# Fused attention and experts: the later pairs' softmax reciprocals turned on VectorE and sent through DRAM instead of through TensorE

## Chip, cores and metric

One Trainium2 chip, one core. The metric is the device time of one execution in microseconds (us); smaller is better. The core has five engines, each with its own queue of instructions that is worked off in order: TensorE (PE in the profile, its weight loads PEld), VectorE (DVE), ScalarE (ACT), GpSimd (POOL) and SyncE (SP), which here only issues transfers.

## The reference, cut to what matters

```python
def _attn_ref(q, k, v, f):                       # 4 batches, 8 heads, 576 tokens, 64 dims
    scores = np.matmul(q, k.transpose(0, 1, 3, 2)) / np.sqrt(D)
    cum = np.cumsum(np.log(np.clip(f, 0.0001, 1.0)), axis=-1)
    scores = np.where(causal, -1e9, scores + cum[:, :, :, None] - cum[:, :, None, :])
    attn = np.exp(scores - np.max(scores, axis=-1, keepdims=True))
    attn = attn / (np.sum(attn, axis=-1, keepdims=True) + 1e-09)
    return np.matmul(attn, v)

def _moe_ref(x, domain_probs, w1, w2):           # 2304 tokens of 512, 4 experts of 1024
    p = domain_probs / (domain_probs.sum(-1, keepdims=True) + 1e-09)
    for e in range(4):
        out += p[:, e:e + 1] * (np.maximum(x @ w1[e], 0.0) @ w2[e])
```

The change concerns the division by the row sums. The kernel multiplies the unscaled product of the weights and v by the reciprocal of each query's sum. That product lies transposed, head dimension on the partitions and queries along the free axis, while the sums come with one query per partition, so the reciprocals have to be turned.

## The kernel before

Work is cut into "pairs" of two heads: 4 batches x 4 pairs x 2 halves of the queries (half 0: queries 0 to 255, half 1: queries 256 to 575) make 32 pairs, in the order of `JOBS` (L35). The four pairs of batch 0, half 0 are handled by the class `First` in a start-up phase written in a fixed order (`startup`, L1064). The other 28 (12 of half 0, 16 of half 1) are handled by `Job`, and their steps are interleaved with the expert steps: the main loop (L1166) records one expert step of a 256-token chunk after another and calls `pace` (L1052), which records attention steps up to a share of the work given by costs. A scheduler then sets each engine's final order; the order of recording alone doesn't fix it.

For one head of a pair, `head_steps` (L667) records: the split of the inputs in a high and a low part (`prep`), per tile of 128 queries the scores on PE, a running minimum on DVE and the exponential on ACT with the row sum as a by-product (`qk_tile`, L415), and one head later the turning of the weights (`tr`, L497: transposes on PE, high part copied by ACT at L475, low part by DVE at L482) and the product with v (`av`, L544: matmuls at L515, ACT copy `tmp` at L529, DVE sum `xs` at L537). After the second head of a pair, `recip` (L420) and later `fin` (L549) do the scaling:

- `recip`: DVE adds 1e-9 to the sums (L422) and takes the reciprocal (L425), 128 partitions x 4 or 6 values; POOL spreads each value to 64 columns (`rb`, L427).
- `fin` calls `spread` (L432): PE turns `rb` with one transpose per query tile (L437), two for half 0 and three for half 1, into a PSUM tile `b` out of the four of `ps_a`, which the scores, turned weights and products also use. Then DVE multiplies `xs` by `b` (L556 or L579), and the result is split into `xh` and `xl` (L562, L565) or written to `xf`.

```python
def spread(self):                                                  # L432
    ps = ps_a.tile([128, 512], F32, tag="a", name=f"b{self.nm}")
    for t in self.its:
        i, o = t - self.its[0], TOK0[t] - self.q0
        nc.tensor.transpose(
            ps[:, o : o + 128], self.rb[:, i].rearrange("p h d -> p (h d)"), ident
        )
    self.r = ps
```

The expert part consists of two sweeps over the chunks (`Step`, L748: first product L764, gate on ACT L775 and DVE L776, second product L794, weighted sum on DVE L816) and, at the end, 16 steps on the last four chunks together (`Big`, L921: L934, L960, L961, L992). Weights are split in a high part by ACT (L731) and a low part by POOL (L736). All transfers are issued by SP: weights L714, raw inputs L276, decay rows L295 read back from a DRAM tile `ncd` that was written at L200.

Of the kernel before, what the change touches and what calls it, by code (L numbers as in the profile page):

```python
# [8 lines left out]
F32 = mybir.dt.float32  # L9
F32R = mybir.dt.float32r  # L10
AF = mybir.ActivationFunctionType
ALU = mybir.AluOpType
# [57 lines left out]
def fused(ctx: ExitStack, tc: tile.TileContext, qk, v, f, probs, w, out):  # L70
# [33 lines left out]
    prob = const.tile([128, NT // 128, E], F32, name="prob")  # L104
    psum_ = const.tile([128, NT // 128, 1], F32, name="psum_")
    warm = const.tile([B * H, 1], F32, name="warm")
    ncd = dr_p.tile([B * H, 2, S], F32, tag="ncd", name="ncd", bufs=1)

    scr = acc_p.tile([128, 1024], F32, tag="acc", name="scr")
# [33 lines left out]
    def decays():  # L143
# [22 lines left out]
            channel_multiplier=1,  # L166
        )
        make_identity(nc, ident)
        for i in jobs[1:NPR]:
            nc.gpsimd.memset(i.kq[64:65, :, :CH], 8.0)  # L170
        for t in q2:
# [82 lines left out]
    class Job:  # L254
# [95 lines left out]
        def begin(self, hh):  # L350
            for t in self.its:
                self.p[hh, t] = p_p.tile([128, S], F32, tag="p", name=f"p{self.nm}_{hh}_{t}")
            self.nmax[hh] = st_p.tile([128, 8], F32, tag="nmax", name=f"nm{self.nm}_{hh}")
            if hh == 0:
                n = len(self.its)
                self.ssum = st_p.tile([128, 2, n], F32, tag="ssum", name=f"ss{self.nm}")
                self.rs = st_p.tile([128, 2, n], F32, tag="rs", name=f"rs{self.nm}")

        def qk_pe(self, hh, its):

# [59 lines left out]
        def recip(self):  # L420
            n, w_ = len(self.its), self.wq
            nc.vector.tensor_scalar(  # L422
                out=self.ssum, in0=self.ssum, scalar1=1e-9, scalar2=None, op0=ALU.add
            )
            nc.vector.reciprocal(out=self.rs, in_=self.ssum)  # L425
            self.rb = x_p.tile([128, 3, 2, D], F32, tag="r", name=f"rb{self.nm}")
            nc.gpsimd.tensor_copy(  # L427
                out=self.rb[:, :n],
                in_=self.rs.rearrange("p h i -> p i h").unsqueeze(3).to_broadcast([128, n, 2, D]),
            )  # L430

        def spread(self):  # L432

            ps = ps_a.tile([128, 512], F32, tag="a", name=f"b{self.nm}")
            for t in self.its:
                i, o = t - self.its[0], TOK0[t] - self.q0
                nc.tensor.transpose(  # L437
                    ps[:, o : o + 128], self.rb[:, i].rearrange("p h d -> p (h d)"), ident
                )
            self.r = ps  # L440

        def blocks(self):

# [28 lines left out]

        def tr_hi(self, hh, gi):
            ps, a0, first, at = self.tp[hh, gi]
            nc.scalar.activation(  # L475
                out=self.pt[hh][0][:, a0 : a0 + at - first], in_=ps[:, first:at], func=AF.Copy
            )

# [18 lines left out]
        def tr(self, hh, gi):  # L497
            self.tr_pe(hh, gi)
            self.tr_hi(hh, gi)
            self.tr_lo(hh, gi)  # L500

        def av_pe(self, hh):
            w_ = self.wq
# [45 lines left out]
        def fin(self):  # L549
# [1 line left out]
            pieces = place(self.b, self.half)  # L551
            k = self.pr
            direct = any(p[1] in DIRECT for p in pieces)
            self.spread()
            if direct:
                nc.vector.tensor_tensor(  # L556
                    out=self.xs[:, :w_], in0=self.xs[:, :w_], in1=self.r[:, :w_], op=ALU.mult
                )
            for d, c, o, n in pieces:
                if c in DIRECT:  # L560
                    th, tl = x_tiles(c)
# [9 lines left out]
                else:  # L571
# [4 lines left out]
                            out=xf[c][:, k, o : o + n], in_=self.xs[:, d : d + n]  # L576
                        )
                    else:
                        nc.vector.tensor_tensor(  # L579
                            out=xf[c][:, k, o : o + n],  # L580
                            in0=self.xs[:, d : d + n],
                            in1=self.r[:, d : d + n],
                            op=ALU.mult,
                        )


    class First(Job):
# [35 lines left out]
        def av_pe(self, hh):  # L623
# [3 lines left out]
            for jt, (a, z) in enumerate(((0, 256), (256, 384))):  # L627
# [4 lines left out]
                    start=(jt == 0),  # L632
                    stop=(jt == 1),
                )

        def spread_out(self):
            self.spread()
# [606 lines left out]
```

## Time and profile before

| what | value |
|---|---|
| median of 3 runs | 977.1 us (lowest 976.92, highest 1357.05) |
| the profiled execution's own time | 976.83 us |
| its span (first to last instruction) | 975.0 us, so 1.83 us lie around it |
| granted TensorE clock, mean | 0.999 of full speed |

The profile page gives per engine the busy time as a share of the span. A group of instructions is named by its line, engine and tile names; a wait names the instruction that waited and the one that released it. PE matmuls overlap in the records (each lasts longer than the step to the next one's start), so what one costs in the queue is read from the difference of start times.

### The profile page before, as it was taken

The numbers are of one execution on the slowest core, as the hardware profiler recorded it, in microseconds if no ns is written. First come the engines' busy times: TensorE is split into PE (matmuls) and PEld (weight loads), VectorE is DVE, ScalarE is ACT, GpSimd is POOL, SyncE is SP. The second block draws the span as 40 slices with busy tenths as digits, with TensorE's granted clock in tenths as the row PEclk, the third lists the DMA queues.
The fourth block names the chain that finished last, engine by engine and source line by source line (L and its number), as shares of the span: only waits on it lengthen the run. The fifth ranks groups of instructions, "written<-read, shape, count | busy, mean of one in ns | idle before, by whom it ended". The sixth has DMA issues, their size and how long they took to land.

```text
span 975.0 us, 15448 instructions
## 1 busy us (share of the span) xinstructions
PE 963.2 (99%) x5690; PEld 848.1 (87%) x5690; DVE 657.3 (67%) x1349; ACT 472.0 (48%) x979; POOL 413.0 (42%) x459
## 2 busy tenths in 40 slices
PE   8999999999999999999999999999999999999998
PEld 6898999899999999999899999988788888888886
DVE  6876565777867878877777563247866666566665
ACT  7776665566556656666556353234333232323220
POOL 4987763502303202204104083477654444555410
PEclk9999999999999999999999999999999999999999
DMA  7665331332412212313412022322211112111002
GB/s 258 255 207 163 118 106 49 103 109 69 137 52 90 102 54 84 120 52 96 150 57 66 23 66 83 113 86 66 87 44 44 44 43 69 62 44 44 23 0 87
DMA packets 29819, 85.87 MB, mean 88 GB/s; under 512 B 3160, under 2 KB 5264, under 8 KB 29744
## 3 DMA queue, kind: packets, MB, share of 16 engines
q1 hardware_dynamic: 29744, 84.89, 26.8%
q8 instruction: 45, 0.74, 0.3%
q14 instruction: 30, 0.25, 0.1%
HBM read 80.00 MB, written 4.87 MB: 87 GB/s over the span
## 4 chain that ended last, share of the span: by engine, by line
PE 87%; POOL 4%; DVE 3%; issue 2%; DMA 2%; ACT 1%; POOLq 0%; ACTq 0%; DVEq 0%
PE l L764 21%; PE l L794 20%; PE y L992 17%; PE m L934 13%; PE s L377 5%; PE t L465 5%; PE o L515 5%; POOL bwl L914 2%; DMA wr<-in_w 1%; POOL wt L891 1%; PE b L437 1%; POOL wl L736 1%; DVE kl L333 1%; DVE hi L339 0%; ACT wh L731 0%
## 5 line engine op out<-in xcount | busy, mean ns | idle before, releaser
L736 POOL TENSOR_TENSOR wl<-wr,wh 128x512 fp32r<-128x512 f32 x114 | 150.3, 1344 | 76.6 <-ACT wh L731 63.0
L764 PE MATMUL l<-xl,wh 128*128 128x256 f32 x640 | 182.0, 285 | 0.3 <-DVE xl L658 0.3
L764 PE MATMUL l<-xh,wh 128*128 128x256 f32 x640 | 181.2, 284 | 0.2 <-ACT xh L657 0.2
L764 PE MATMUL l<-xh,wl 128*128 128x256 f32 x640 | 181.3, 284 | 0.0
L816 DVE SCALAR_TENSOR_TENSOR acc<-y,prob,acc 128x512 f32<-128x512 f32 x120 | 88.3, 746 | 68.5 <-PE y L992 68.5
L406 ACT ACTIVATE p<-p,nm 128x576 f32<-128x576 f32 (+2 forms) x160 | 96.0, 600 | 64.8 <-DVE nm L391 64.3
L794 PE MATMUL l<-wh,gh 128*128 128x512 f32 x320 | 127.2, 398 | 0.0
L794 PE MATMUL l<-wl,gh 128*128 128x512 f32 x320 | 127.1, 397 | 0.0
L794 PE MATMUL l<-wh,gl 128*128 128x512 f32 x320 | 126.0, 396 | 0.0
L764 PEld LDWEIGHTS l<-xh,wh 128*128 128x128 f32 x640 | 120.5, 188 | 3.2 <-ACT xh L657 0.4
L764 PEld LDWEIGHTS l<-xl,wh 128*128 128x128 f32 x640 | 120.6, 188 | 3.0 <-DVE xl L658 0.5
L764 PEld LDWEIGHTS l<-xh,wl 128*128 128x128 f32 x640 | 120.5, 188 | 0.5
L325 POOL CAST q<-raw 64x320 fp32r<-64x320 f32 (+1 forms) x56 | 26.9, 480 | 210.3 <-PE s L377 181.9
L914 POOL TENSOR_TENSOR bwl<-wr,bwh 128x256 fp32r<-128x256 f32 (+1 forms) x80 | 78.5, 1009 | 80.5 <-ACT bwh L911 80.5
L391 DVE CUSTOM_DVE_ANT_0 p<-s,mask 128x288 f32<-128x288 f32 (+2 forms) x160 | 75.6, 477 | 43.3 <-PE s L377 39.7
L992 PE MATMUL y<-bwh,hh 128*128 128x512 f32 x256 | 101.1, 395 | 0.8 <-DVE acc L816 0.8
L992 PE MATMUL y<-bwl,hh 128*128 128x512 f32 x256 | 101.1, 395 | 0.0
L992 PE MATMUL y<-bwh,hl 128*128 128x512 f32 x256 | 100.4, 395 | 0.0
L776 DVE SCALAR_TENSOR_TENSOR gl<-l,gh 128x512 fp32r<-128x512 f32 x80 | 54.9, 686 | 54.6 <-ACT gh L775 54.4
L482 DVE TENSOR_TENSOR ptl<-t,pth 128x320 fp32r<-128x320 f32 (+2 forms) x120 | 65.3, 553 | 37.0 <-ACT pth L475 36.6
L934 PE MATMUL m<-rl,bwh 128*128 128x512 f32 x224 | 87.5, 390 | 0.0
L934 PE MATMUL m<-rh,bwh 128*128 128x512 f32 x224 | 87.3, 390 | 0.0
(117 smaller groups left out, 2077.5 us busy)
## 6 DMA issues: line engine op xcount, KB each, us to landing
wr<-in_w SPq DMA_DIRECT2D x96, 512.0 KB
raw<-in_qk SPq DMA_DIRECT2D x16, 896.0 KB
raw<-in_qk SPq DMA_DIRECT2D x12, 512.0 KB
vr<-in_v SPq DMA_DIRECT2D x16, 320.0 KB
out<-acc SPq DMA_DIRECT2D x16, 256.0 KB
vr<-in_v SPq DMA_DIRECT2D x8, 128.0 KB
first<-in_qk SPq DMA_DIRECT2D x3, 256.0 KB
first<-in_v SPq DMA_DIRECT2D x4, 128.0 KB
```

Source lines behind the costliest of these rows:

```text
L377: nc.tensor.matmul(out=ps[:, at : at + z - a], lhsT=lhsT, rhs=rhs, start=(m == 0), stop=(m == 1),)
L391: nc.vector.tensor_tensor_reduce(out=pt[:, a:z], in0=ps, in1=mask[:, m0 + a : m0 + z], scale=-0.125, scalar=BIG if n == 0 else nm[:, col : ...
L406: return nc.scalar.activation(out=pt[:, :w_], in_=pt[:, :w_], func=AF.Exp, scale=-1.0, bias=self.nmax[hh][:, c : c + 1], accum_out=self.ss ...
L482: nc.vector.tensor_tensor(out=lo[:, a0 + first : a0 + at - first], in0=ps[:, 2 * first : at], in1=hi[:, a0 + first : a0 + at - first].bitc ...
L736: eng.tensor_tensor(out=wl[n][:, a:z], in0=wraw[n][:, a:z], in1=wh[n][:, a:z].bitcast(F32), op=ALU.subtract)
L764: nc.tensor.matmul(out=self.l1p[:, fi, :], lhsT=lhsT, rhs=rhs[:, k, :], start=(k == 0 and m == 0), stop=(k == 3 and m == 2),)
L776: nc.vector.scalar_tensor_tensor(out=self.gl, in0=self.l1p, scalar=0.0, in1=self.gh.bitcast(F32), op0=ALU.max, op1=ALU.subtract,)
L794: nc.tensor.matmul(out=l2[tt], lhsT=lhsT, rhs=rhs, start=(self.ps == 0 and fi == 0 and m == 0), stop=(self.ps == 1 and fi == 1 and m == 2),)
L816: nc.vector.scalar_tensor_tensor(out=acc[c][:, tt, :], in0=ps, scalar=sc, in1=acc[c][:, tt, :], op0=ALU.mult, op1=ALU.add,)
L914: nc.gpsimd.tensor_tensor(out=lo[:, a:z], in0=x[:, a:z], in1=hi[:, a:z].bitcast(F32), op=ALU.subtract)
L934: nc.tensor.matmul(out=ps, lhsT=lhsT[:, o], rhs=rhs[:, k, :], start=(k == 0 and i == 0), stop=(k == 1 and i == 2),)
L992: nc.tensor.matmul(out=ps, lhsT=lhsT, rhs=rhs, start=(fi == 0 and m == 0), stop=(fi == 1 and m == 2),)
```

## The change

For the 28 later pairs the turning of the reciprocals leaves PE and POOL. `widen` has DVE write the 4 or 6 reciprocals per partition into the first columns of a constant 128 x 32 tile `rs32` (two of them, used in turn, filled with ones by POOL at the start), transpose it in blocks of 32 by 32 into `rt`, and ScalarE issues a transfer of `rt` to a DRAM tile `rd` in which all 128 queries of a head and query tile lie in a row. `fetch`, recorded after the last high-part copy of the second head's turned weights (`self.tail`), has ScalarE issue the read back: each head's row of 128 n values goes to 64 partitions of `r` in SBUF. `fin` then multiplies by `r`; since the third query tile overlaps the second by 64 queries, `scale` cuts at column 256 and half 1 pairs take a second instruction there. The four `First` pairs keep the old path.

```diff
--- before.py
+++ after.py
@@ -104,6 +104,7 @@
     prob = const.tile([128, NT // 128, E], F32, name="prob")
     psum_ = const.tile([128, NT // 128, 1], F32, name="psum_")
     warm = const.tile([B * H, 1], F32, name="warm")
+    rs32 = [const.tile([128, 32], F32, name=f"rs32_{n}") for n in range(2)]
     ncd = dr_p.tile([B * H, 2, S], F32, tag="ncd", name="ncd", bufs=1)
 
     scr = acc_p.tile([128, 1024], F32, tag="acc", name="scr")
@@ -166,6 +167,8 @@
             channel_multiplier=1,
         )
         make_identity(nc, ident)
+        for t in rs32:
+            nc.gpsimd.memset(t, 1.0)
         for i in jobs[1:NPR]:
             nc.gpsimd.memset(i.kq[64:65, :, :CH], 8.0)
         for t in q2:
@@ -354,7 +357,6 @@
             if hh == 0:
                 n = len(self.its)
                 self.ssum = st_p.tile([128, 2, n], F32, tag="ssum", name=f"ss{self.nm}")
-                self.rs = st_p.tile([128, 2, n], F32, tag="rs", name=f"rs{self.nm}")
 
         def qk_pe(self, hh, its):
 
@@ -422,22 +424,29 @@
             nc.vector.tensor_scalar(
                 out=self.ssum, in0=self.ssum, scalar1=1e-9, scalar2=None, op0=ALU.add
             )
-            nc.vector.reciprocal(out=self.rs, in_=self.ssum)
-            self.rb = x_p.tile([128, 3, 2, D], F32, tag="r", name=f"rb{self.nm}")
-            nc.gpsimd.tensor_copy(
-                out=self.rb[:, :n],
-                in_=self.rs.rearrange("p h i -> p i h").unsqueeze(3).to_broadcast([128, n, 2, D]),
-            )
-
-        def spread(self):
-
-            ps = ps_a.tile([128, 512], F32, tag="a", name=f"b{self.nm}")
-            for t in self.its:
-                i, o = t - self.its[0], TOK0[t] - self.q0
-                nc.tensor.transpose(
-                    ps[:, o : o + 128], self.rb[:, i].rearrange("p h d -> p (h d)"), ident
+            self.widen()
+
+        def widen(self):
+            n, x = len(self.its), rs32[self.pr % 2]
+            nc.vector.reciprocal(
+                out=x[:, : 2 * n].rearrange("p (h i) -> p h i", h=2), in_=self.ssum
+            )
+            rt = st_p.tile([128, 32], F32, tag="rt", name=f"rt{self.nm}", bufs=2)
+            nc.vector.transpose(out=rt, in_=x)
+            self.rd = dr_p.tile([32, 4, 32], F32, tag="rd", name=f"rd{self.nm}")
+            nc.scalar.dma_start(out=self.rd.rearrange("c b r -> b c r"), in_=rt)
+
+        def fetch(self):
+            n = len(self.its)
+            self.r = x_p.tile([128, 384], F32, tag="r", name=f"r{self.nm}")
+            with tc.issue_after(self.tail.ins):
+                nc.scalar.dma_start(
+                    out=self.r[:, : 128 * n],
+                    in_=self.rd[: 2 * n]
+                    .rearrange("(h i) b r -> h (i b r)", h=2)
+                    .unsqueeze(1)
+                    .to_broadcast([2, 64, 128 * n]),
                 )
-            self.r = ps
 
         def blocks(self):
 
@@ -472,7 +481,7 @@
 
         def tr_hi(self, hh, gi):
             ps, a0, first, at = self.tp[hh, gi]
-            nc.scalar.activation(
+            self.tail = nc.scalar.activation(
                 out=self.pt[hh][0][:, a0 : a0 + at - first], in_=ps[:, first:at], func=AF.Copy
             )
 
@@ -498,6 +507,8 @@
             self.tr_pe(hh, gi)
             self.tr_hi(hh, gi)
             self.tr_lo(hh, gi)
+            if hh == 1 and gi == len(self.blocks()) - 1:
+                self.fetch()
 
         def av_pe(self, hh):
             w_ = self.wq
@@ -551,11 +562,8 @@
             pieces = place(self.b, self.half)
             k = self.pr
             direct = any(p[1] in DIRECT for p in pieces)
-            self.spread()
             if direct:
-                nc.vector.tensor_tensor(
-                    out=self.xs[:, :w_], in0=self.xs[:, :w_], in1=self.r[:, :w_], op=ALU.mult
-                )
+                self.scale(self.xs, 0, w_)
             for d, c, o, n in pieces:
                 if c in DIRECT:
                     th, tl = x_tiles(c)
@@ -576,12 +584,17 @@
                             out=xf[c][:, k, o : o + n], in_=self.xs[:, d : d + n]
                         )
                     else:
-                        nc.vector.tensor_tensor(
-                            out=xf[c][:, k, o : o + n],
-                            in0=self.xs[:, d : d + n],
-                            in1=self.r[:, d : d + n],
-                            op=ALU.mult,
-                        )
+                        self.scale(xf[c][:, k, o : o + n], d, n)
+
+        def scale(self, out, d, n):
+            for a, z, o in ((d, min(d + n, 256), 0), (max(d, 256), d + n, 64)):
+                if a < z:
+                    nc.vector.tensor_tensor(
+                        out=out[:, a - d : z - d],
+                        in0=self.xs[:, a:z],
+                        in1=self.r[:, a + o : z + o],
+                        op=ALU.mult,
+                    )
 
 
     class First(Job):
@@ -632,6 +645,24 @@
                     start=(jt == 0),
                     stop=(jt == 1),
                 )
+
+        def widen(self):
+            rs = st_p.tile([128, 2, 2], F32, tag="rs", name=f"rs{self.nm}", bufs=2)
+            nc.vector.reciprocal(out=rs, in_=self.ssum)
+            self.rb = x_p.tile([128, 2, 2, D], F32, tag="r", name=f"rb{self.nm}")
+            nc.gpsimd.tensor_copy(
+                out=self.rb,
+                in_=rs.rearrange("p h i -> p i h").unsqueeze(3).to_broadcast([128, 2, 2, D]),
+            )
+
+        def spread(self):
+
+            ps = ps_a.tile([128, 512], F32, tag="a", name=f"b{self.nm}")
+            for i in range(2):
+                nc.tensor.transpose(
+                    ps[:, 128 * i : 128 * i + 128], self.rb[:, i].rearrange("p h d -> p (h d)"), ident
+                )
+            self.r = ps
 
         def spread_out(self):
             self.spread()
```

The scheduler sets the order anew. On PE, at the end of pair 1 of batch 0, half 1 (`o0_1_1_1` is its last product, `b0_1_1` the turned reciprocals, `l1` and `l2` are expert products, `t0_2_1` the next pair's weights being turned), the order before:

```order
L515 MATMUL o0_1_1_1_2894<-pth0_1_1_1_2791,v20_1_1_2269 128x192
L515 MATMUL o0_1_1_1_2894<-ptl0_1_1_1_2792,v20_1_1_2269 128x192
L515 MATMUL o0_1_1_1_2894<-pth0_1_1_1_2791,v20_1_1_2269 128x64
L437 MATMUL b0_1_1_2906<-ident_108,rb0_1_1_2732 128x128 x3
L764 MATMUL l1_1_0_1_1_4047<-xh1_620,wl34_3921 128x256
L764 MATMUL l1_1_0_1_1_4047<-xh1_620,wh34_3920 128x256
L465 MATMUL t0_2_1_0_0_2938<-ident_108,p0_2_1_0_2_2760 128x128
```

and now:

```order
L526 MATMUL o0_1_1_1_2900<-pth0_1_1_1_2795,v20_1_1_2272 128x192
L526 MATMUL o0_1_1_1_2900<-ptl0_1_1_1_2796,v20_1_1_2272 128x192
L526 MATMUL o0_1_1_1_2900<-pth0_1_1_1_2795,v20_1_1_2272 128x64
L474 MATMUL t0_2_1_0_0_2941<-ident_108,p0_2_1_0_2_2765 128x128
L474 MATMUL t0_2_1_0_0_2941<-ident_108,p0_2_1_0_3_2766 128x128
L825 MATMUL l2_0_7_2_0_0_3723<-wl29_2711,gh0_7_2_0_3620 128x512
L825 MATMUL l2_0_7_2_0_0_3723<-wh29_2710,gl0_7_2_0_3621 128x512
```

The row of three transposes is gone, and the products of the expert step that stand behind it are of an earlier step (sweep 0, group 7, chunk 2 instead of sweep 1, group 0, chunk 1). On ACT, from the exponential of this pair's last tile (`p0_1_1_1_4`) on, the order before (`wh` are weights being split, `tmp` a copy of a product):

```order
L406 ACTIVATE p0_1_1_1_4_2588,ss0_1_1_2428<-p0_1_1_1_4_2588,nm0_1_1_1_2589 128x576
L529 ACTIVATE tmp0_1_1_2756<-o0_1_1_0_2746 64x320
L406 ACTIVATE p0_2_1_0_2_2760,ss0_2_1_2764<-p0_2_1_0_2_2760,nm0_2_1_0_2763 128x384
L731 ACTIVATE wh34_3920<-wr34_3176 128x1024
L731 ACTIVATE wh35_3927<-wr35_3287 128x1024
L475 ACTIVATE pth0_1_1_1_2791<-t0_1_1_1_0_2793 128x512
L475 ACTIVATE pth0_1_1_1_2791<-t0_1_1_1_1_2816 128x384
L475 ACTIVATE pth0_1_1_1_2791<-t0_1_1_1_2_2854 128x320
L406 ACTIVATE p0_2_1_0_3_2761,ss0_2_1_2764<-p0_2_1_0_3_2761,nm0_2_1_0_2763 128x512
L775 ACTIVATE gh1_0_1_0_3970<-l1_1_0_1_0_3934 128x512
```

and now, with the write of the turned reciprocals (`rd0_1_1`) and the read (`r0_1_1`):

```order
L408 ACTIVATE p0_1_1_1_4_2591,ss0_1_1_2433<-p0_1_1_1_4_2591,nm0_1_1_1_2592 128x576
L806 ACTIVATE gh0_7_2_0_3620<-l1_0_7_2_0_3582 128x512
L540 ACTIVATE tmp0_1_1_2761<-o0_1_1_0_2751 64x320
L408 ACTIVATE p0_2_1_0_2_2765,ss0_2_1_2769<-p0_2_1_0_2_2765,nm0_2_1_0_2768 128x384
L437 DMA rd0_1_1_2737<-rt0_1_1_2735 4x32x32
L484 ACTIVATE pth0_1_1_1_2795<-t0_1_1_1_0_2797 128x512
L484 ACTIVATE pth0_1_1_1_2795<-t0_1_1_1_1_2820 128x384
L484 ACTIVATE pth0_1_1_1_2795<-t0_1_1_1_2_2858 128x320
L443 DMA r0_1_1_2864<-rd0_1_1_2737 128x1x384
L408 ACTIVATE p0_2_1_0_3_2766,ss0_2_1_2769<-p0_2_1_0_3_2766,nm0_2_1_0_2768 128x512
L806 ACTIVATE gh0_7_2_1_3719<-l1_0_7_2_1_3649 128x512
```

The write stands behind the gate, one copy and one exponential of the next pair, the read right behind the three copies of turned weights (`pth0_1_1_1`); two weight splits that stood there before have moved elsewhere.

## Rows read from the trace of the kernel before

**Rows 1.** The page's head and busy time of each engine.

```profile
span 975.0 us, 15448 instructions
...
PE 963.2 (99%) x5690; PEld 848.1 (87%) x5690; DVE 657.3 (67%) x1349; ACT 472.0 (48%) x979; POOL 413.0 (42%) x459
```

**Rows 2.** Busy time by stretch; columns: stretch, its length, engines, clock, DMA share, GB/s.

```profile
30.00:100.00 70.00, 69.12 (x474) 63.33 (x474) 54.27 (x127) 50.09 (x112) 60.31 (x69) 1.00 0.57 189
100.00:180.00 80.00, 80.00 (x558) 74.04 (x557) 46.01 (x123) 47.88 (x118) 47.07 (x57) 1.00 0.29 86
...
700.00:800.00 100.00, 100.00 (x434) 81.30 (x433) 63.58 (x92) 30.01 (x52) 49.93 (x55) 1.00 0.16 53
```

**Rows 3.** Waits of PE; columns: who <- whom, us in total, times, longest.

```profile
PE b L437 <- POOL rb L427: 1.1, 1, 1.1
PE y L992 <- DVE acc L816: 0.8, 1, 0.8
PE o L515 <- DVE ptl L482: 0.7, 1, 0.7
PE s L377 <- DVE nm L391: 0.5, 1, 0.5
```

**Rows 4.** PE in order of time around the `b` of a half 1 pair; columns: start, length.

```profile
248.46 0.55 PE L437 MATMUL b<-ident,rb 128*128 128x128 f32 x3
248.77 0.36 PE L764 MATMUL l<-xh,wl 128*128 128x256 f32 x1
248.97 0.28 PE L764 MATMUL l<-xh,wh 128*128 128x256 f32 x1
249.09 0.38 PE L465 MATMUL t<-ident,p 128*128 128x128 f32 x2
```

**Rows 5.** The same around the `b` of a half 0 pair.

```profile
204.58 0.41 PE L437 MATMUL b<-ident,rb 128*128 128x128 f32 x2
204.74 0.37 PE L764 MATMUL l<-xh,wl 128*128 128x256 f32 x1
204.94 0.28 PE L764 MATMUL l<-xh,wh 128*128 128x256 f32 x1
```

**Rows 6.** Groups by line; columns: operation, tiles, count, busy us, mean ns, idle before.

```profile
L437 PE MATMUL b<-ident,rb 128*128 128x128 f32 x80 | 15.2, 286 | 1.1 <-POOL rb L427 1.1
...
L565 DVE TENSOR_TENSOR xl<-xs,xh 128x256 fp32r<-128x256 f32 x16 | 8.5, 530 | 2.1 <-ACT xh L562 1.9
...
L425 DVE RECIPROCAL rs<-ss 128x4 f32<-128x4 f32 (+1 forms) x32 | 5.7, 179 | 1.4
```

**Rows 7.** Transfers issued by SP: nanoseconds of an issue, shortest, median, longest.

```profile
L295 SPq DMA_DIRECT2D kl<-ncd x56: 221/251/443, 20.2 to 513.7; - x56
...
L276 SPq DMA_DIRECT2D raw<-in_qk x28: 545/546/612, 11.9 to 505.8; - x28
```

**Rows 8.** The chain of work that ended last, its first transfer: start, length.

```profile
0.73 1.91 DMA scr<-in_f
```

**Rows 9.** SP's queue in order of time: a write to DRAM and its read back.

```profile
14.55 0.31 SPq L200 DMA_DIRECT2D ncd<-scr  x1
...
20.17 0.53 SPq L295 DMA_DIRECT2D kl<-ncd  x2
```

**Rows 10.** ACT in order of time for the pair of rows 4.

```profile
236.87 0.19 ACT L406 ACTIVATION_READ_ACCUMULATOR p<-p,nm 128x1 f32 x1
...
241.04 1.53 ACT L475 ACTIVATE pth<-t 128x512 fp32r<-128x512 f32 x3
```

**Rows 11.** DVE in order of time for the same pair.

```profile
238.69 0.17 DVE L425 RECIPROCAL rs<-ss 128x6 f32<-128x6 f32 x1
...
251.59 0.49 DVE L537 TENSOR_TENSOR xs<-o,tmp 64x320 f32<-64x320 f32 x1
```

**Rows 12.** DVE in order of time, one instruction at 460 us.

```profile
460.06 4.30 DVE L333 TENSOR_TENSOR kl<-raw,hi 64x576 fp32r<-64x576 f32 x1 [0.80 <-ACT hi L324]
```

**Rows 13.** POOL in order of time at the same place.

```profile
459.96 3.77 POOL L736 TENSOR_TENSOR wl<-wr,wh 128x512 fp32r<-128x512 f32 x3
```

## Prediction

> **What bounds the kernel now.** I read the page's head and busy times first [rows 1]: PE is busy 963.2 of 975.0 us, the next engine, DVE, 67%. That alone doesn't prove a bound, since matmul records overlap, so next came the busy time by stretch [rows 2]: from 30 us on PE loses at most about 0.9 us in a stretch, at clock 1.00, whether DVE and ACT are loaded to 78% and 72% (30 to 100 us) or less (58% and 60% from 100 to 180). Third, the waits of PE [rows 3]: the longest entries are 1.1, 0.8, 0.7 and 0.5 us, once each. Fourth, PE in order of time [rows 4, 5]: one instruction starts as soon as the one ahead lets it. So the program is one long queue on PE with almost no holes, and a change is worth what it takes out of that queue, less the holes it makes. The other engines count only where they get so late that PE has to wait.
>
> **The change part by part.** The sum is made against the profiled execution, 976.83 us (span 975.0 and 1.83 around it).
>
> *Transposes off PE.* 28 pairs lose their `b` transposes: 12 pairs with two, 16 with three, 72 of the 80 in the group of line 437 [rows 6]. The mean of 286 ns in that row is the length of a record, not what it takes from the queue; the starts tell that. In a half 1 pair three transposes start at 248.46, and the second expert product behind them starts at 248.97; one product takes 0.12 (248.97 to 249.09), so the three take 248.97 - 248.46 - 0.12 = 0.39 us, in which the slower change from transposing back to products is contained [rows 4]. In a half 0 pair it is 204.94 - 204.58 - 0.12 = 0.24 us [rows 5]. The sum: 16 x 0.39 + 12 x 0.24 = 6.2 + 2.9 = 9.1 us off PE. All of it lies on the queue that sets the end, so I take it whole: -9.1. Where a transpose of weights follows directly, some of the price of changing stays; that makes it a little less, not another case.
>
> *POOL.* 28 copies `rb` go, and two small fills come at the start; POOL is at 42% and nobody but PE waited for these copies, for 1.1 us in one case [rows 1, 3]. That one is in the start-up phase, where the four `First` pairs stay as they are. Zero.
>
> *DVE.* 28 block transposes come. The trace shows none; the nearest rows are the reciprocal at 179 ns and a two-input product over 256 columns at 530 ns [rows 6], and I take 0.2. The multiplication now reads `r` in SBUF in place of PSUM, and half 1 pairs get a second piece. With 0.2 to 0.5 us more for each of some 70 instructions DVE gets 14 to 35 us more of 975, and goes from 67% to about 70%. Off the path.
>
> *ACT.* Two issues per pair, 56 in all. SP's issues take 0.25 us (two rows, median) to 0.55 us (128 partitions, two heads) [rows 7]; 56 times that is 14 to 31 us of ACT's queue, spread over the 527 us between 30 and 557. In the stretch 100 to 180 ACT goes from 60% to about 65%. What stands behind an issue in the queue are exponentials, copies of turned weights and the gates; a gate is needed only after the next step's 24 products (24 x 0.12 = 2.9 us), which covers one issue several times. Zero, with up to 31 us if nothing covered it.
>
> *The write's wait.* ACT stands at the write until the block transpose is done. In the pair shown the sums were complete at 237.06 (236.87 + 0.19) and the reciprocal at 238.86 [rows 10, 11]; the transpose ends some 0.3 later, and in the new order a gate, a copy and an exponential of the next pair stand between on ACT. Hidden but for some tenths.
>
> *The read's wait.* ACT stands at the read until the write has landed. No row shows a write of this size. A read of 2 KB took 1.91 us from the start of its issue [rows 8]; that is the lower bound. A 72 KB write issued at 14.55 held back its own read until 20.17, 5.6 us, with larger loads under way [rows 9]; the upper. From the reciprocal's end at 238.86 to the end of the last turned weights at 242.57 (241.04 + 1.53) there are 3.7 us [rows 10, 11]. I take the value nearest to the smaller transfer, some 2.2 with the issue: it is over when ACT reaches the read. With 5.6 ACT would stand 2 us in each pair, which is the second rival.
>
> *The read's landing.* From 242.57 to the end of the last sum `xs` at 252.08 (251.59 + 0.49) are 9.5 us in which the read has to arrive [rows 10, 11]; with the same bounds it does. The Trainium skill (DMA: Bandwidth & Descriptors, section on why a DMA increments its semaphore by 16) speaks against this read: the number of DMA engines is the largest up to 16 that divides the first dimension on both sides, here 2 for two heads. By its 436 GB/s for all 16, an estimate for 192 KB on two is 2.0 + 3.6 = 5.6 us in place of 2.4. No run here shows it yet; by the one and by the other the 9.5 us hold, and only the second rival's chance is raised by it.
>
> *A denser order.* Beside the 72 transposes the new order runs attention ahead: at the pair shown, PE's queue stands in an expert step five places earlier than before. The half 0 pairs thus get closer together, roughly to what the stretch from 30 to 100 us looks like, where PE lost 0.88 us in 70 [rows 2]. From 100 to 180 us it lost nothing. I add 80 / 70 x 0.88 = +1.0. Below is zero (DVE and ACT may keep up), above the first rival.
>
> *DVE behind POOL.* A DVE product with both inputs in SBUF lasted 4.30 us, until 464.36, while three POOL products ran until 463.73 [rows 12, 13]; soon after it PE waited 0.5 us for the minimum `nm` [rows 3]. The new scaling is such a two-input product, 28 pairs and the second pieces. I add one further wait of the longer kind, 0.7 [rows 3]. The Trainium skill (SBUF — State Buffer, section on who interferes with whom) says that a DVE instruction with two SBUF inputs is blocked for a whole GpSimd instruction that reads SBUF, and the reverse; the trace agrees, with 4.30 us. With PSUM as one input, as `b` was, it doesn't apply, so the rule speaks against this part; read strictly it could strike at each of the new products, and then the first rival is where it leads.
>
> Sum: 976.83 - 9.1 + 1.0 + 0.7 = 969.4 us. The median is 0.27 above the profiled execution, so 969.7.
>
> **The rivals.**
> 1. *The gain is eaten by density.* If all of 30 to 557 us ran with the losses of the stretch 30 to 100, PE would lose 527 / 70 x 0.88 = 6.6 us [rows 2] in place of the 1.0: 976.83 - 9.1 + 6.6 + 0.7 = 975.0. For it: ACT and DVE both get more work, in less time. Against it: from 100 to 180 us neither is above 60%, and PE's lead over the gates is a whole step.
> 2. *ACT stands at the read and PE waits (slower).* It holds the read until the write has landed, and gates, exponentials and turned weights queue behind it. It decides from the point at which a write takes longer than the 3.7 us of rows 10 and 11. With the 5.6 of rows 9 ACT stands 2 us in each pair; if PE then waits as long as in its longest wait for a late vector result, 0.7 [rows 3], it is 28 x 0.7 = 19.6: 976.83 - 9.1 + 19.6 = 987.3. For it: a queue in order, and 28 round trips through DRAM. Against it: rows 9 come from the start, when all inputs are loaded; later the DMA share is 0.29 and 0.16 [rows 2].
> 3. *The late waits go too.* The order is new, so the waits of 0.7 and 0.5 need not come again, and the added 1.7 neither: 976.83 - 9.1 - 1.2 = 966.5.
>
> **How the numbers follow.** Chances: the forecast 0.58, rival 1 0.20, rival 2 0.15, rival 3 0.07. The range 964.5 to 980 holds the forecast and rivals 1 and 3 with a little on either side and leaves out most of rival 2. 2% is about what a measurement of this kernel can tell from no change, and it is 19.5 us: faster than 957.6 would need more than the transposes and all waits since 30 us together, 0.01; slower than 996.6 only a rival 2 with 1 us of PE per pair, 0.04; within 2% 0.95.
>
> **What would show it.** Right: PE has 72 fewer instructions of line 437 and its busy time is about 9 us less, with no new entry above 1 us among PE's waits; ACT's waits for the write are under 1 us a pair; DVE's scaling doesn't wait for the read. Wrong: a row in which ACT waits for the transfer of `rd` by microseconds, many times, with PE waiting for `gl` or `ptl` behind it; scaling instructions of 2 us and more beside POOL's; or a time that is lower by less than 5 us although no wait on PE has grown, which would mean that the transposes cost less than the starts say.

## The result and the profile after

The changed kernel takes 983.55 us (median of seven, 980.59 to 988.49) against 978.95 for the kernel before in the same comparison: the ratio is 1.0053, 95% interval 1.0027 to 1.0078 (a ratio of means, in which one execution of the kernel before that took 1357.05 us is left out). It is slower by about 5 us where 7.4 us less had been forecast (969.4 against 976.83). The profiled execution is the slowest of the seven (988.49 us), so its waits are somewhat larger than usual.

The page's head and busy times of the changed kernel, against [rows 1]:

```profile
span 986.7 us, 15439 instructions
...
PE 969.9 (98%) x5618; PEld 852.3 (86%) x5618; DVE 667.9 (68%) x1393; ACT 469.4 (48%) x979; POOL 398.7 (40%) x433
```

The 72 transposes are gone (5690 to 5618 instructions), and yet PE is busy for longer. Busy time by stretch, against [rows 2]:

```profile
30.00:100.00 70.00, 66.88 (x448) 60.34 (x447) 55.30 (x115) 45.93 (x101) 56.00 (x60) 1.00 0.61 196
100.00:180.00 80.00, 76.53 (x513) 70.71 (x513) 54.70 (x150) 49.57 (x132) 45.54 (x56) 0.96 0.32 101
700.00:800.00 100.00, 100.00 (x434) 81.37 (x433) 66.57 (x96) 30.97 (x54) 50.52 (x56) 1.00 0.17 54
```

From 30 to 180 us PE got through 961 matmuls where before it got through 1032, with 6.6 us idle instead of 0.9, and the granted clock fell to 0.96 in the second stretch. From 700 to 800 us PE does the same as before. Between the end of the attention and there the place of the tiles tells, of which more below. PE's waits, against [rows 3]:

```profile
PE o L526 <- DVE ptl L491: 3.2, 3, 2.3
PE l L795 <- ACT xh L570: 2.0, 1, 2.0
...
PE b L662 <- POOL rb L653: 1.1, 1, 1.1
PE t L474 <- ACT p L408: 1.0, 2, 0.5
PE t L474 <- DVE nm L393: 0.8, 1, 0.8
```

The new entries are late results of DVE (turned weights, minima) and ACT (scaled activations, exponentials), not the transfers themselves. The transfers show one step further back. The two lines that issue them (nanoseconds: shortest, median, longest), the write first:

```profile
L437 ACTq DMA_DIRECT2D rd<-rt x28: 539/540/1113, 49.7 to 557.4; - x28
```

```profile
L443 ACTq DMA_DIRECT2D r<-rd x28: 535/536/562, 52.8 to 561.7; - x28
L443 ACTq EVENT_SEMAPHORE  x22: 17/17/2449, 64.8 to 561.6; - x22
```

Each of the 56 issues takes ACT 0.54 us in the median, 30.9 us in all. The gaps on ACT right in front of the 28 reads add up to 12.8 us, 2.46 us in the longest. ACT stands in front of the writes as well: 27 of the 28 are issued 0.03 us after the block transpose that they wait for has ended, and the gaps in front of them add up to 19.8 us, 3.68 us in the longest, and are above 1 us in eight. The longest, on ACT and then on DVE:

```profile
475.42 0.58 ACT L806 ACTIVATE gh<-l 128x512 fp32r<-128x512 f32 x1
479.69 0.54 ACTq L437 DMA_DIRECT2D rd<-rt  x1
...
479.46 0.20 DVE L435 STREAM_TRANSPOSE rt<-rs 128x32 f32<-128x32 f32 x1
```

How long the transfers are shows in the chain of work that ended last (start, length):

```profile
63.86 4.20 DMA rd<-rt
84.95 7.16 DMA r<-rd
95.13 4.08 DMA rd<-rt
99.28 4.56 DMA r<-rd
...
278.47 5.32 DMA rd<-rt
...
347.62 8.59 DMA r<-rd
...
409.31 5.71 DMA rd<-rt
415.12 8.37 DMA r<-rd
```

On this chain, which holds seven of the writes and four of the reads, a write needs 3.9 to 5.7 us from its issue, a read 4.6 to 8.6. The longest wait on PE, at 77 us, looks like this on DVE and POOL in order of time:

```profile
74.94 2.59 DVE L315 TENSOR_TENSOR v<-vb,v 128x128 fp32r<-128x128 f32 x2
77.45 1.83 DVE L592 TENSOR_TENSOR xs<-xs,r 128x256 f32<-128x256 f32 x1
79.32 0.56 DVE L491 TENSOR_TENSOR ptl<-t,pth 128x384 fp32r<-128x384 f32 x1
...
71.04 6.34 POOL L767 TENSOR_TENSOR wl<-wr,wh 128x512 fp32r<-128x512 f32 x5
...
77.75 1.25 POOL L767 TENSOR_TENSOR wl<-wr,wh 128x512 fp32r<-128x512 f32 x1
```

The new multiply of line 592 lasts 1.83 us beside POOL (0.42 in the median), and the turned weights for which PE stands come right behind it. At 103 us it is ACT, and then the clock:

```profile
103.00 0.38 PE L474 MATMUL t<-ident,p 128*128 128x128 f32 x2
105.41 0.50 PE L795 MATMUL l<-xh,wh 128*128 128x256 f32 x2 [2.03 <-ACT xh L570]
```

```profile
103.00:115.00 12.00, 9.42 (x49) 8.66 (x48) 5.93 (x19) 6.04 (x19) 3.17 (x6) 0.72 0.24 71
115.00:127.00 12.00, 12.00 (x84) 11.10 (x83) 7.56 (x23) 8.95 (x19) 9.91 (x11) 1.00 0.48 153
```

Behind that stall of 2.0 us, and another of 0.5 us at 106 us, PE ran at its lower level, 1.2 GHz, until about 113 us (a 256-column product takes 0.21 us from start to start instead of 0.12); the mean granted clock of the 12 us is 0.72.

So four suspects stood: the scheduler's new order, the multiply beside POOL, the round trip through DRAM, and, from the fourth experiment on, something that slows the expert matmuls.

### The profile page after: what moved, and what is told of

Read it like the earlier page. It is cut to its first block, busy times and chain, and to the rows that moved or that the text cites. A ratio compares the mean times of both kernels' runs of the same rounds, so it can differ in the third digit from the quotient of the medians.

```text
span 986.7 us, 15439 instructions
## 1 busy us (share of the span) xinstructions
PE 969.9 (98%) x5618; PEld 852.3 (86%) x5618; DVE 667.9 (68%) x1393; ACT 469.4 (48%) x979; POOL 398.7 (40%) x433
## 4 chain that ended last, share of the span: by engine, by line
PE 76%; DVE 10%; DMA 6%; issue 3%; ACT 2%; POOL 1%; ACTq 0%; DVEq 0%; POOLq 0%
PE y L1023 17%; PE l L825 16%; PE l L795 16%; PE m L965 14%; PE s L379 4%; PE t L474 4%; PE o L526 3%; DMA rd<-rt 3%; DMA r<-rd 3%; DVE wl L767 1%; DVE v L315 1%; DVE p L393 1%; DVE ss L424 1%; DVE acc L847 1%; PE s L608 1%
## 5 line engine op out<-in xcount | busy, mean ns | idle before, releaser
L795 PE MATMUL l<-xh,wh 128*128 128x256 f32 x640 | 183.7, 288 | 2.0 <-ACT xh L570 2.0
```

Source lines behind the costliest of these rows:

```text
L795: nc.tensor.matmul(out=self.l1p[:, fi, :], lhsT=lhsT, rhs=rhs[:, k, :], start=(k == 0 and m == 0), stop=(k == 3 and m == 2),)
```

## The experiments

Ratios are to the kernel before, with 95% intervals; a difference of two ratios is put into us by 978.4, its median. To hold an engine to an order, each of its instructions was tied behind its forerunner in a list taken from the other kernel, with an edge that orders issue alone:

```diff
+            for a, z in zip(order, order[1:]):
+                tc.add_manual_dep(z, a.name, NOSYNC, reason="in_order")
```

No run does this to a kernel with its own order and changes nothing else. The nearest is e6 below, the changed kernel in its own order without one of its waits, which stands within 0.0004 of it.

**e1, e2: order and work exchanged.**

> The changed kernel's operations, with every engine held to the order that the kernel before had (the 72 transposes and the 28 copies on GpSimd simply missing from it); only the 56 transfers on ScalarE's queue are placed by the scheduler. Theory order (the closer order of batch 1's attention takes away the slack in front of PE): the 9.1 us of the transposes come back nearly whole, ratio to before 0.990 to 0.994, about 969 to 972 us. Theory lock (VectorE's multiply now reads two SBUF operands and stands behind GpSimd): the 56 multiplies are all still there, so ratio 1.003 to 1.006. Theory round trip (write 4 to 6 us, read 5 to 9 us, VectorE and ScalarE held): the trips are as long as before and only somewhat better covered, ratio 0.999 to 1.004.

> The other half of the crossing: the operations of the kernel before (transposes on PE, widening on GpSimd, factors in PSUM, no round trip), with every engine held to the changed kernel's order; the 72 transposes and 28 GpSimd copies are placed by the scheduler. Theory order: about as much is lost as the changed kernel lost beyond its gain, 10 to 14 us, ratio to before 1.010 to 1.015. Theory lock and theory round trip: neither is in this kernel, ratio 0.998 to 1.003.

e1: 1.0126 (1.0107 to 1.0146). e2: 1.0058 (1.0041 to 1.0074). The new order, with none of the new work, costs the old work 5.7 us (its 72 transposes and 28 copies placed by the scheduler): theory order was right on e2 in its direction, with a number about twice too large. But the old order doesn't help the new work, it makes it worse, which none of the theories had. ACT and then PE in order of time in e1 show one place where it does:

```profile
98.33 0.54 ACTq L683 DMA_DIRECT2D rd<-rt  x1
...
103.83 0.55 ACTq L689 DMA_DIRECT2D r<-rd  x1
104.42 0.51 ACT L654 ACTIVATE p<-p,nm 128x256 f32<-128x256 f32 x1 [4.11 <-DMA rd<-rt]
...
105.07 0.44 PE L721 MATMUL t<-ident,p 128*128 128x128 f32 x2 [1.87 <-ACT p L654]
```

The write is issued at 98.33, the read stands until it has landed, and ACT is idle for 4.11 us before the exponential behind the read, for which PE waits 1.9 us.

**e3 to e5: without the transfers.** In e3 and e5 `fetch` sets `self.r = one`, an SBUF tile of ones, and both transfers go; e3 in the new order, e5 in the old. e4 is e3 with one operand:

```diff
-                    nc.vector.tensor_tensor(
+                    nc.vector.tensor_scalar(
                         out=out[:, a - d : z - d],
                         in0=self.xs[:, a:z],
-                        in1=self.r[:, a + o : z + o],
-                        op=ALU.mult,
+                        scalar1=0.001,
+                        scalar2=None,
+                        op0=ALU.mult,
```

> The changed kernel in the changed kernel's own order, without the 28 writes and 28 reads: the multiply takes its second operand from an SBUF tile of ones instead (the softmax division is left out; reciprocal and block transpose stay). Theory round trip: what the trips hold up is gone, about 969 to 974 us, ratio to before 0.990 to 0.995. Theory order and theory lock: the order and the multiply with two SBUF operands are as in the changed kernel, ratio 1.002 to 1.006.

> As the run without transfers, in the same order, and the multiply is by a constant: one SBUF operand instead of two (the softmax division is left out). Theory lock: faster than the run without transfers by 3 to 10 us, and the slow multiplies (up to 1.83 us beside GpSimd in the changed kernel) fall to 0.2 to 0.4 us. Theory order and theory round trip: the same as the run without transfers within 2 us.

> The changed kernel's operations in the order of the kernel before, without the 28 writes and 28 reads (the multiply takes a tile of ones; the softmax division is left out). It closes the square of order and transfers: new order with transfers 1.0053, old order with transfers 1.0126, new order without 1.0006. Theory round trip (the transfers are what makes the old order slow): it falls by 12 us or more, ratio 0.990 to 0.998. Theory order as first put (the old order has the slack in front of PE): 3 to 6 us below the new order without transfers, 0.994 to 0.997. If what slows both orders is the multiply or the missing transposes themselves, it stays above 1.003.

e3: 1.0006 (0.9996 to 1.0016); e4: 0.9993 (0.9981 to 1.0005); e5: 1.0005 (0.9991 to 1.0019). The transfers cost 4.6 us in the new order and 11.8 in the old. The second operand is worth 1.3 us as measured, with intervals that overlap, where theory lock had 3 to 10, so it isn't the main cause. With e5 theory order falls in its first form: the old order is no better for the new work than the new one. What none of the theories had: 72 transposes less and no transfers, and still no gain.

**e6, e7: the two waits apart.** e6 keeps all 56 transfers but multiplies by `one`; e7 drops the writes and reads constant rows.

```diff
-                        in1=self.r[:, a + o : z + o],
+                        in1=one[:, a + o : z + o],
```

> The changed kernel in its own order with all 56 transfers as they are, but VectorE's multiply takes a tile of ones and so waits for no read (the softmax division is left out). Only ScalarE is still held, at each read's issue until its write has landed. Theory held (the trip's price is ScalarE standing at the read): as slow as the changed kernel, ratio 1.004 to 1.006. Theory landing (the price is VectorE waiting for the read to land): as the run without transfers, 0.999 to 1.002.

> The changed kernel in its own order without the 28 writes; each read fetches the same constant rows of DRAM, written once near the start, so that ScalarE never stands at a read, and VectorE's multiply waits for the read's landing as in the changed kernel (the softmax division is left out). Theory held: as the run without transfers, ratio 0.999 to 1.002. Theory landing: as slow as the changed kernel, 1.003 to 1.006.

e6: 1.0057 (1.0041 to 1.0074), as slow as the whole change; e7: 0.9973 (0.9960 to 0.9985). So the price of the transfers lies on ACT, and DVE's wait for the landing (10.8 us in eight places in the changed kernel) costs nothing there, since e6 has none of it. e7 says less on that, as DVE waits for only 4.1 us in it, and its tiles also lie at a better place than e6's (below; by an estimate from the last 400 matmuls some 1.5 of the 8.2 us between the two). What it does show is that 28 read issues on ACT alone cost nothing: what is dear comes with the writes. These two runs don't part their issues, ACT's standing in front of them until the block transpose is done, and its standing at the reads until the writes have landed.

**e8: two reads.**

```diff
+                for h in range(2):
                     nc.scalar.dma_start(
-                        out=self.r[:, : 128 * n],
+                        out=self.r[64 * h : 64 * h + 64, : 128 * n],
```

> The changed kernel in its own order, each read issued as two, one per head with 64 rows, the second right behind the first on ScalarE's queue. If the long landing (4.6 to 8.6 us) comes from the read's outermost count of two, the two reads land in 2.5 to 4 us, and by theory landing the ratio falls to 1.000 to 1.003. Theory held: the landing does not matter, and 28 more issues of 0.54 us on ScalarE leave it at 1.005 to 1.008.

1.0105 (1.0081 to 1.0128), above both theories. DVE waits for no read any more, so two reads do land sooner (in e17, below, which has two as well, those on the chain take 2.7 and 3.1 us), and yet the time rises by 5 us, with 28 further issues on ACT and with gaps of 15.7 us in front of the reads. The Trainium skill (DMA: Bandwidth & Descriptors, section on why a DMA increments its semaphore by 16) has the count of DMA engines follow from the first dimension on both sides, two for one read of both heads; the 8.6 us of one read and the missing waits with 64 rows agree in direction. No run here shows the count itself.

**e9, e10, e13, e16: the place of the tiles.** After the attention all kernels run the same expert matmuls, but not equally fast. The changed kernel's new small tiles in front move all later ones up. e9 does only that to the kernel before:

```diff
+    const.tile([128, 448], mybir.dt.uint8, name="pad")
     ncd = dr_p.tile([B * H, 2, S], F32, tag="ncd", name="ncd", bufs=1)
```

e10 pads the changed kernel by 576 bytes, e13 the run e3 by 64, e16 the kernel before by 320.

> The kernel before with one unused SBUF tile of 448 bytes per partition ahead of the work pools and nothing else: the same instructions in the same order, but the split weights (wh, wl) and all tiles behind them lie 448 bytes further up, where the changed kernel's new small tiles put them (704 becomes 128 modulo 1024). New theory place: in the stretch after the attention, where both kernels run the same expert matmuls, the last 400 of them take 62.8 us in the kernel before and in the run with the new order (address 192 modulo 512), 63.3 us in the run with reads alone (256) and 63.8 us in the changed kernel and the five other runs (128); if it is the address, these 400 take 63.8 us here, the 1920 first-layer matmuls lose about 0.003 us each, 5 to 6 us in all, ratio 1.004 to 1.007. If it is not the address, 62.8 us and ratio 0.999 to 1.001.

> The changed kernel with one unused SBUF tile of 576 bytes per partition, which brings the weights' address back to 704 modulo 1024, as in the kernel before; instructions and order as in the changed kernel. Theory place: the last 400 expert matmuls in 62.8 us instead of 63.8 and 5 to 6 us less in all, ratio to before 0.998 to 1.001. Without it: 1.004 to 1.006 as the changed kernel.

> The run without transfers (new order, multiply by ones, the softmax division left out) with 64 unused bytes more, so that the weights' address is 704 modulo 1024 as in the kernel before. So far that run stands at 1.0006 though 72 transposes are gone from it. If place is what took the gain back, it gives 3 to 4 us here: ratio 0.996 to 0.998, and the sum closes: about 8.6 us for the transposes, less 4.7 us for the order (the run with the new order), 974 us. If instead PE's saved time only turns into longer waits for VectorE and ScalarE (as the shifted changed kernel suggests, which stayed at 1.0064), 0.999 to 1.001.

> The kernel before with 320 unused bytes: the weights at address 0 modulo 512. Theory place gives no number for an address not yet seen; of the three seen the last 400 expert matmuls took 62.8 us (192), 63.3 (256) and 63.8 (128). If multiples of 128 are what is bad (128 and 256 against 192), 63.3 to 63.8 us and ratio 1.002 to 1.004; if being aligned to 512 is good, under 62.8 us and 0.996 to 1.000.

e9: 1.0032 (1.0019 to 1.0045); e10: 1.0064 (1.0048 to 1.0079); e13: 0.9975 (0.9962 to 0.9987); e16: 1.0000 (0.9986 to 1.0013). The last 60 us of expert matmuls, busy time and PE's count first, in the kernel before, e9, the changed kernel and e10:

```profile
577.06:637.06 60.00, 60.00 (x383) 54.27 (x381) 18.65 (x25) 18.59 (x27) 31.08 (x27) 1.00 0.30 97
```

```profile
582.30:642.30 60.00, 60.00 (x378) 54.35 (x378) 18.72 (x25) 17.61 (x26) 30.10 (x27) 1.00 0.30 97
```

```profile
589.33:649.33 60.00, 60.00 (x376) 54.23 (x375) 18.57 (x25) 17.53 (x26) 29.49 (x27) 1.00 0.29 97
```

```profile
582.45:642.45 60.00, 60.00 (x383) 54.27 (x382) 18.49 (x25) 17.81 (x27) 30.23 (x26) 1.00 0.29 97
```

At full clock and with no waits, 383 matmuls fit with the weights at 192 modulo 512, and 376 to 378 with them at 128, whichever kernel it is; 448 unused bytes make the kernel before 3.1 us slower, of 5 to 6 expected. Only the 256-column products are affected: among the last 400 matmuls one takes 0.117 us from start to start in the kernel before and 0.120 in e9, and a 512-column product 0.229 and 0.230. e13 against e3 gives 3.0 us for the same. In e10, where ACT is held, the faster matmuls bring nothing; that miss isn't explained. At address 0 (e16) and 256 (e7) the last 400 matmuls take 63.3 us, between the 62.8 and the 63.8 of the others, but e16 as a whole is no slower than the kernel before.

**e11, e12: the read on SyncE.** The read by `nc.sync`, e11 in the changed kernel's order, e12 in a new one of the scheduler, both at the old address.

> The changed kernel in its own order, shifted by 576 bytes as in the run before this one, and the 28 reads issued by SyncE instead of ScalarE, so that ScalarE neither stands there until the write has landed (12.8 us over 28 reads in the changed kernel) nor pays 0.54 us for each issue. Theory held: as the run with only the read awaited and at the better address, ratio 0.992 to 0.997. If SyncE's own queue makes the reads late or holds its loads: as the shifted changed kernel or worse, 0.999 to 1.004.

> As the run before this one, but the scheduler orders everything anew with the reads on SyncE. Theory held: 0.992 to 0.997 as well, give or take 0.003 for another order. If the order decides by itself, it departs from the run before this one by more than 0.004.

e11: 1.0059 (1.0045 to 1.0073); e12: 1.0101 (1.0084 to 1.0118); both missed 0.992 to 0.997. In e11 SyncE's queue stands instead, and a load of raw inputs behind it comes late; the waits of SyncE and of ACT:

```profile
SPq L676 <- DMA rd<-rt: 131.3, 28, 17.7
```

```profile
ACT hi L560 <- DMA raw<-in_qk: 6.0, 1, 6.0
```

**e14, e15, e17: a later read.** e14 puts each read up to three instructions later on ACT; e17 up to two, and as two reads; e15 puts read and multiply later in the program and leaves the order to the scheduler. All at the old address.

> The shifted changed kernel (1.0064), its own order but for ScalarE's, where each read stands three instructions later or right behind the pair's last copy of the numerators, so that the write has more time to land before ScalarE comes to the read. Theory held: the gaps in front of the reads fall from 12.8 us to under 3 us and the ratio to 0.996 to 1.000. If the later read makes VectorE wait for its landing and that counts too: 1.000 to 1.006.

> A version meant to be kept: the changed kernel at the old address, the read issued behind the pair's last copy of the numerators, and the multiply one tile step later (behind the first tile of the next pair's head), the scheduler's own order. Theory held: neither ScalarE nor VectorE waits for a transfer, ratio 0.992 to 0.997. If a new order costs by itself what the first one did: 1.000 to 1.006.

> Both ends of the trip at once, in the changed kernel's order at the old address: the read stands two ScalarE instructions later (so that ScalarE is not held; with three and one read the gaps fell from 12.8 to 0.6 us, but VectorE then waited 56.8 us for the landing) and is issued as two, one per head (so that it lands sooner; in the run with two reads VectorE waited for none). Theory both ends: gaps before the reads under 5 us, VectorE's waits for the reads under 10 us, ratio 0.998 to 1.004. If two reads land no sooner than one, VectorE waits 20 us or more and the ratio stays above 1.012.

e14: 1.0273 (1.0249 to 1.0297); e15: 1.0259 (1.0234 to 1.0283); e17: 1.0054 (1.0033 to 1.0075). In e14 the gaps before the reads fall from 12.8 to 0.6 us as meant, and DVE pays:

```profile
DVE xf L827 <- DMA r<-rd: 40.7, 12, 5.8
DVE xs L827 <- DMA r<-rd: 16.1, 9, 2.6
```

With 56.8 us of standing on DVE the time is 20 us above e10's, where DVE stands for 8.7 us; in e15, which missed its range as well, it stands for 75.3 us. In e17 both are short, no gap and 5.1 us on DVE, in its profiled and fastest execution (977.47 us; the others up to 987.75). What is left on ACT are the 84 issues, 46.6 us, and the gaps in front of the writes, 18.0 us; which of them is the rest of the price isn't shown. A rival stands untested there: e11 and e17 take ACT's standing at the reads away and stay at 1.005 to 1.006, each with a price of its own, and in both ACT still stands in front of the writes for 18 us. No run takes that alone away.

**e18: second halves only**, with two reads, at the old address; `widen` and `spread` of the first halves as before.

> A version meant to be kept: only the 16 pairs of the second halves (three transposes each, 0.39 us, 6.2 us in all) go through DRAM, with two reads; the 12 pairs of the first halves widen on GpSimd and transpose on PE as in the kernel before; the old address; the scheduler's own order. Theory both ends: the stretch up to 180 us is as in the kernel before, the second halves have 25 us per pair and hide most of the trip, ratio 0.996 to 1.001. If the order and ScalarE's issues cost there too what they cost in the changed kernel: 1.001 to 1.006.

1.0005 (0.9995 to 1.0016): as fast as the kernel before, with 48 of its 80 transposes gone. No version that does the division beat the kernel before.

## Why the prediction was wrong, point by point

Five steps lead from one kernel to the other:

| step | from, to | ratio | us |
|---|---|---|---|
| the new order | before, e2 | 1 to 1.0058 | +5.7 |
| transposes and copies off, DVE's part on | e2, e13 | to 0.9975 | -8.1 |
| tiles 128 instead of 192 modulo 512 | e13, e3 | to 1.0006 | +3.0 |
| transfers on ACT | e3, e6 | to 1.0057 | +5.0 |
| DVE waits for the landing | e6, after | to 1.0053 | -0.4 |

It adds up to the whole by the way it is built; what is shown are the parts, each with an uncertainty of 1.6 to 3 us. The third is borne out by e9 (+3.1). They hold along this path only: by them e10 would stand at 1.002, e5 at 0.995, and neither does. That time which PE saves becomes a longer wait where ACT or DVE sets the pace is the likely reason; it is argued, not shown.

- *Transposes off PE*, -9.1, taken whole: right in size in one order only. In the new order -8.1 was measured, with the new multiply and the block transpose (0.206 us, 0.2 taken) in it. In the old order the same step at one address, from e9 to e5, gives -2.6. The profiled executions show a part of the difference there: from 30 to 557 us PE is idle for 3.2 us in e5 and 1.8 in e9, and the granted clock from 100 to 180 us is 0.98 in e5 and 1.00 in e9.
- *ACT*, taken as zero with 31 us as the upper bound of its duration: the duration was that bound, 0.54 us an issue and 30.9 us in all. The cover was argued from the gates alone; what came late were exponentials and the scaled activations. This step failed: with the standing of the next two points it cost 5.0 us.
- *The write's wait*, "hidden but for some tenths", failed: ACT stands at 27 of the 28 writes until the block transpose is done, with gaps of 19.8 us in all. What that costs by itself no run shows.
- *The write's size* failed: 2.2 us taken as the nearest to the smaller transfer, 3.9 to 5.7 measured. The value lay near the upper bound, 5.6. With it ACT stands at the read, 12.8 us in all, as the second rival has it; the rival's price, 0.7 us of PE per pair and 19.6 in all, was four times too large even if the whole 5.0 us of the transfers were due to it.
- *The read's landing*, 2.4 us taken, was 4.6 to 8.6. DVE waited for it in eight places, 10.8 us, against "the 9.5 us hold", but e6 shows that this cost nothing. The second estimate given there, 5.6, was nearer and still short.
- *A denser order*, +1.0 by scaling one stretch's loss to another: +5.7 measured. This step failed too. It took the loss as idle time of PE spread evenly, but in e2's profiled execution PE is idle for 4.1 us from 30 to 557 us against 2.1 before, which is 2.0 of the 4.7 us by which that execution is longer; where the rest lies stays open. The first rival's 6.6 for density is near in size, by the same reasoning and so by luck.
- *DVE behind POOL*, +0.7: within what e4 allows. The Trainium skill's rule (SBUF — State Buffer, who interferes with whom) shows at 77 us, 1.83 us beside POOL; on the whole it is small.
- *The place of the tiles*, +3.0, was no step at all.

The range failed because the rivals were taken as alternatives. Order, ACT and, along this path, place came together and outweighed the gain.

## What to carry to other kernels

A round trip through DRAM is priced on the queue that issues it: both issues, and the standing in front of each, at the slow bound; moving the read later only hands the wait to its reader, another queue hands it to that queue's loads. Before a gain or loss of half a per cent is put down to an edit, hold the order and the tiles' addresses fixed, since each moved this kernel by 3 to 6 us without any work changed. Time taken off the busiest engine is worth what the new order, and the engines that feed it, leave of it: of 9.1 us here the best run, with the division left out, kept 2.6 (e7).

## What was not expected of the hardware

- Matmuls of 256 columns run up to 3% slower or faster (0.117 or 0.120 us) by where their tiles start in SBUF, in the sum 3 us of 978 (e9). Why, and whether it is the weights or another of the shifted tiles, was not tried.
- After stalls of 2.0 and 0.5 us on PE at 103 and 106 us of the changed kernel the granted clock was 0.50 from 106.5 to 113.2 us, by an estimate some 3 us lost. The longer stall at 77 us, 2.3 us, left it at 1.00.
- The same eight score matmuls near 8.9 us take 1.55 us in e5 and 2.70 in e3, with the same instructions: whether the clock is up by then differs from execution to execution. The first expert matmul starts at 24.8 to 27.7 us for it.

Open: why e10 gains nothing from the better address, what takes most of 5 us from e5 in the old order, where nothing is transferred, and which part of ACT's work on the transfers is the dear one.
